# Four orders ahead of the first feed-forward product, and new priorities behind it, in a fused attention and Fourier-mixing kernel

## The chip, the cores and the metric

The kernel runs on one core of one Trainium2 chip. The metric is the device time of one execution in microseconds (us), lower is better. The core has four engines that compute side by side, TensorE (PE in the profile), VectorE (DVE), ScalarE (ACT) and GpSimd (POOL), and a fifth, SyncE (SP), which here only issues transfers. Each engine works through its own list of instructions in the order in which they were written; where one needs another's result, it waits on a semaphore.

## The reference

Eight batches of 448 tokens with 12 heads of 64. Cosine attention, then a Fourier mixing over tokens and channels of which only the real part is kept, then a layer norm and a two-layer feed-forward with a residual:

```python
q_n = q / (np.linalg.norm(q, axis=-1, keepdims=True) + 1e-06)
k_n = k / (np.linalg.norm(k, axis=-1, keepdims=True) + 1e-06)
scores = np.matmul(q_n, k_n.transpose(0, 1, 3, 2)) / tau        # tau = 0.1
attn = softmax(scores)
x = np.matmul(attn, v)            # heads joined: (8, 448, 768), float32
mixed = np.real(fft(fft(x, axis=1), axis=2))
u = x + mixed
un = (u - mean(u)) / np.sqrt(var(u) + 1e-06)
out = u + np.maximum(un @ w_ch1, 0.0) @ w_ch2     # 768 -> 3072 -> 768
```

## The kernel before

The whole program is written down first as a list of steps (`P.add`, each with its engine or engines to choose from, an estimated duration, a priority, what it reads and writes), and a planner (`Plan.schedule`) then deals the steps out: whenever an engine comes free it takes, of the steps that are ready by the planner's own clock, the one with the lowest priority number. The result is one fixed list per engine. In that list only true dependences become semaphore waits (`deps`). A second kind of relation, `order`, only says that one step may be dealt out after another has been; it sets places in the lists and never makes a wait.

A table `SHIFT` adds a number to the priority of single steps by name and occurrence (`"mask": {0: 513.4649}`). It was found by a search, so there is nothing to read in its numbers; their effect is the order of the lists.

The work of one batch b, with the names of its steps:

- Loads of q, k, v. Squares of q and k on ACT (`sqK`, `sqQ`, `sqT`; T is the tail of 64 tokens), their sums on DVE (`ssK`, `ssQ`, `ssT`), logarithm and exponential for the root on ACT (`ln`, `nrm`), and the scaling of q and k on DVE (`scK`, `scQ`, `scT`). For batches 0 and 1 the scaled tiles are transposed on PE (`tk`, `tq`, `tt`) through two PSUM banks (pool "M") and copied out on ACT or DVE (`ek`, `eq`, `et`). From batch 2 on POOL does the scaling and a transfer does the transposing.
- Scores on PE (`qk`), exponentials on ACT (`ex`), values on PE (`pv`), division on DVE (`rd`, `x`), folds of the token axis on DVE (`fa`, `f0`, `f1`, `g`).
- First Fourier product on PE (`fs0`, `fs1`), copied out (`te0` on ACT; for batch 0 `te1` is split, one half on ACT, one on DVE), second one on PE (`fd0`, `fd1`). The sine and cosine tables for it are made on ACT (`sind`), with `mask`, a small DVE step, behind it. In batch 0 the tables are brought into another shape afterwards (`cd0` to `cd5`, `halfd`).
- The residual sum `u` (`u0`, `u1`) for three token tiles on DVE, the tile's negative mean (`ba`), its sum of squares on ACT (`bs`), root (`ln2`, `rs`), the normed tile on DVE (`un`). In batch 0 the first tile is only centred (its root is applied at the very end), so that it needs `ba` but not `bs`. The tile is transposed on PE (`tn0`, in two halves) and copied out of PSUM in two halves (`eu00`, `eu01`).
- The first feed-forward product on PE (`h0` to `h23`, 6 matmuls each; for batch 0 first on the lone first tile, 144 matmuls of 128x128, then on a pair of tiles, 128x256), the ReLU out of pool "M" on ACT or DVE (`relu`), the second product on PE (`y`, and `m1` to `m7` in a form with fewer multiplications), the closing additions on DVE (`fin`), for part of the tiles as a copy on ACT (`fa`, `fv`, `fm`) and an addition on POOL (`fap`, `fvp`, `fmp`), the store by SP or POOL.

The attention of batch b+1 is interleaved with the feed-forward of batch b. PE's idle places before the first product are filled with matmuls whose result nobody reads (`warm`, 6 each). Two switches of ACT's function table stand near the first product: `ldt1` ahead of the sine tables and `ldt` behind them.

The functions that the change touches stand below, with the line numbers of the profile.

Of the kernel before, what the change touches and what calls it, by code (L numbers as in the profile page):

```python
# [86 lines left out]
    "pads": {0: 761.6515}, "sins": {0: 15.0098}, "ldt0": {0: 217.8585}, "ldt1": {0: -55.8965}, "sind": {0: 7.1264}, "mask": {0: 513.4649},  # L87
    "sinp": {0: 701.9659}, "half": {1: 12.0477}, "sinn": {0: -46.2638}, "ldt": {0: 60.769}, "sqK0_0": {0: -198.99}, "ssT0_0": {0: -143.0895},
# [778 lines left out]
def t_act(n, ptr=0):  # L867
    return 0.12 + 0.00089 * n + 0.093 * ptr


def t_dve(n, mode=1):
    return 0.1 + n / (960.0 * mode)
# [15 lines left out]
class Kern:  # L888
# [202 lines left out]
    def first_norm(self, b):  # L1091

        P = self.P
# [7 lines left out]
        if b == 0:  # L1101
            cuts = ((0, 1), (1, 3), (3, 6))
            hf = self.tf[:, 0:10752].bitcast(F32)
            sg = self.hf[:, 0:6144].bitcast(F32)
# [18 lines left out]
        pg = [pr + 1.5 * a for a, _ in cuts]  # L1123
# [1093 lines left out]
```

## Time and profile before

| what | value |
|---|---|
| time, median of 3 runs | 575.67 us (575.16 to 577.59) |
| the profiled execution | 574.34 us, its span 572.5 us |
| PE busy | 552.2 us, 96% of the span |
| DVE busy | 439.6 us, 77% |
| ACT busy | 382.8 us, 67% |
| POOL busy | 231.5 us, 40% |
| granted TensorE clock | 1.00 throughout |
| first feed-forward matmul starts | 48.46 us after the span's start |

A row of the timeline reads: start, length, engine, line, operation, what it writes and reads, and in brackets the idle time before it and who ended it. Rows of one form that follow each other are merged (x2), and their length is then from the first start to the last end. The time an engine is held by an instruction is a little shorter than its length: the next one may start before the last result is written.

### The profile page before, as it was taken

The page shows a single profiled execution, that of the slowest core. Times are in us where ns is not written, and L with a number is a line of the kernel's source. Part 1 is how long each engine was busy: PE and PEld are TensorE (multiplying, and loading weights), DVE is VectorE, ACT ScalarE, POOL GpSimd, SP SyncE. Part 2 cuts the span into 40 slices and gives each one's busy share as a digit, 9 for nine tenths or more (in the row PEclk, how much of TensorE's full clock was granted, in tenths as well). Part 3 has the DMA queues.
Part 4 walks back from the last instruction along what each step waited for, and adds up shares of the span by engine and source line. Part 5 has one row for each costly group of instructions (what it writes and reads, how often), then busy time and mean ns, then how long its engine had stood idle before and what let it go on. Part 6 is the DMA issues. An engine that isn't in the chain of part 4 may idle for free.

```text
span 572.5 us, 15993 instructions
## 1 busy us (share of the span) xinstructions
PE 552.2 (96%) x6598; PEld 432.6 (76%) x6598; DVE 439.6 (77%) x926; ACT 382.8 (67%) x723; POOL 231.5 (40%) x338
## 2 busy tenths in 40 slices
PE   3799999999999999999999999999999999999998
PEld 3569787686787678868778787687786886969695
DVE  8989857988488768886879668977986497987363
ACT  7898895565876676798458775696456752747171
POOL 8534424347345535453471536344532103031303
PEclk9999999999999999999999999999999999999999
DMA  9999998985349938953695549553933100023001
GB/s 193 210 239 174 170 181 123 161 180 109 113 68 114 171 87 126 138 125 92 121 125 109 83 109 132 116 128 54 142 65 34 62 1 26 32 41 73 21 36 56
DMA packets 187897, 62.19 MB, mean 109 GB/s; under 512 B 166800, under 2 KB 185616, under 8 KB 187824
## 3 DMA queue, kind: packets, MB, share of 16 engines
q1 hardware_dynamic: 129856, 38.35, 36.2%
q0 software_dynamic: 57968, 22.81, 36.0%
q8 instruction: 52, 0.85, 0.6%
q14 instruction: 21, 0.17, 0.1%
HBM read 51.90 MB, written 11.01 MB: 110 GB/s over the span
## 4 chain that ended last, share of the span: by engine, by line
PE 75%; DVE 17%; ACT 5%; issue 2%; POOL 1%; DMA 0%; DVEq 0%; POOLq 0%; ACTq 0%
PE PS L1902 26%; PE PS L1758 26%; PE PS L1853 6%; PE PS L1397 6%; PE PS L1360 5%; DVE U L1620 3%; DVE HQ L2002 2%; PE PS L1391 2%; ACT E L1338 2%; PE PS L1373 1%; DVE ACG L1609 1%; PE PS L1525 1%; DVE U L1632 1%; DVE OUTB L1939 1%; DVE SM L1272 1%
## 5 line engine op out<-in xcount | busy, mean ns | idle before, releaser
L1758 PE MATMUL PS<-UNT,W1b 128*128 128x256 bf16 (+1 forms) x1728 | 185.3, 264 | 1.2 <-ACT KTD L1230 0.4
L1758 PEld LDWEIGHTS PS<-UNT,W1b 128*128 128x128 bf16 x1728 | 154.0, 98 | 21.3 <-issue 1.7
L1338 ACT ACTIVATE E<-PS 128x900 bf16<-128x900 f32 (+1 forms) x192 | 149.3, 827 | 28.6 <-PE PS L1360 24.6
L1902 PE MATMUL PS<-W2b,HQ 128*128 128x384 bf16 x720 | 124.8, 326 | 0.0
L1283 POOL TENSOR_TENSOR QH<-STG,SM 128x256 bf16<-128x256 f32 x126 | 87.4, 720 | 90.9 <-DVE SM L1089 64.7
L1928 POOL TENSOR_TENSOR OUTB<-OUTB,U 128x192 f32<-128x192 f32 x72 | 50.8, 725 | 127.0 <-ACT OUTB L1923 125.8
L1902 PEld LDWEIGHTS PS<-W2b,HQ 128*128 128x128 bf16 x720 | 68.8, 98 | 43.3 <-issue 0.6
L1902 PE MATMUL PS<-TX,HQ 128*128 128x384 bf16 (+2 forms) x444 | 76.7, 322 | 1.6 <-DVE OUTB L1939 1.4
L1774 ACT ACTIVATE HQ<-PS 128x512 bf16<-128x512 f32 x82 | 48.8, 597 | 37.9 <-PE PS L1758 37.0
L1902 PEld LDWEIGHTS PS<-TX,HQ 128*128 128x128 bf16 x444 | 41.4, 98 | 28.2 <-DVE OUTB L1939 2.5
L2002 DVE TENSOR_TENSOR HQ<-HQ 128x1536 bf16<-128x1536 bf16 (+1 forms) x73 | 55.1, 758 | 9.1 <-ACT HQ L1774 6.3
L1272 DVE TENSOR_REDUCE SM<-QH 128x6 f32<-128x384 f32 x84 | 45.1, 544 | 13.1 <-ACT QH L1270 12.5
L1397 PE MATMUL PS<-VB,E 128*128 128x65 bf16 x1152 | 51.9, 193 | 0.0
L1270 ACT ACTIVATE QH<-STG 128x384 f32<-128x384 f32 x84 | 43.0, 521 | 10.3 <-DVE SM L1272 9.5
L1397 PEld LDWEIGHTS PS<-VB,E 128*128 128x128 bf16 x1152 | 47.9, 97 | 1.5
L1961 POOL DMA_INDIRECT out_dram<-OUTB,IDX x21 | 23.4, 1115 | 57.5 <-DVE OUTB L1939 30.1
L1774 DVE TENSOR_SCALAR HQ<-PS 128x512 bf16<-128x512 f32 x44 | 30.1, 684 | 19.7 <-PE PS L1758 19.1
L1391 PE MATMUL PS<-VZ,E 128*128 128x130 bf16 x192 | 41.6, 219 | 1.0 <-ACT E L1338 0.9
L1662 ACT ACTIVATE F<-U,MV 128x768 bf16<-128x768 bf16 x28 | 26.2, 934 | 21.2 <-DVE MV L1657 17.8
L1620 DVE SCALAR_TENSOR_TENSOR U<-ACG,X 128x768 bf16<-128x768 f32 (+4 forms) x39 | 39.3, 1014 | 0.7
L1360 PE MATMUL PS<-QK 64*128 64x225 bf16 (+2 forms) x864 | 39.1, 227 | 0.1
L1923 ACT ACTIVATE OUTB<-PS 128x384 f32<-128x384 f32 x36 | 17.6, 488 | 29.5 <-PE PS L1902 29.2
(193 smaller groups left out, 784.3 us busy)
## 6 DMA issues: line engine op xcount, KB each, us to landing
STG<-in_k_dram SPq DMA_DIRECT2D x18, 384.0 KB, 4.6
STG<-in_q_dram SPq DMA_DIRECT2D x18, 384.0 KB, 3.7
VB<-in_v_dram POOLq DMA_DIRECT2D x24, 192.0 KB, 6.7
W1b<-in_moe_w_ch_dram POOLq DMA_DIRECT2D x12, 384.0 KB, 8.0
W2b<-in_moe_w_ch_dram POOLq DMA_DIRECT2D x12, 384.0 KB, 6.7
out_dram<-OUTB SPq DMA_DIRECT2D x7, 384.0 KB, 4.4
W2b<-in_q_dram SPq DMA_DIRECT2D x2, 576.0 KB, 10.1
W2b<-in_k_dram SPq DMA_DIRECT2D x2, 576.0 KB, 11.0
```

Of the source, the lines that this page charges most:

```text
L1272: P.add("dve", lambda v, o=SS[:, i, H // ns * x:H // ns * (x + 1)], sq=sq: v.tensor_reduce(o, sq.rearrange("p (h d) -> p h d", d=DH), AX.X ...
L1283: r = v.tensor_tensor(v3(qh)[:, h:h + 4], v3(buf)[:, h:h + 4], RN[:, i, h:h + 4].unsqueeze(2).to_broadcast((128, 4, DH)), AluOp.mult)
L1338: return a.activation(o, self.PS[:, bk:bk + nc_, 0:SQ2], ACTF.Exp, scale=1.0 / self.tau)
L1360: i = pe.matmul(self.PS[:, bk + h, c0:c0 + n], self.KT[r, jj, kt * 128:(kt + 1) * 128], self.QT[r, jj, cols], start=True, stop=True)
L1391: r = pe.matmul(o, st(6), self.VZ[:, j, :], start=not split, stop=(split and i == 0), skip_group_check=True)
L1397: r = pe.matmul(o[:, 65 * h:65 * h + 65], st(2 * kt + h), self.VB[:, kt, 2 * j + h, :], start=(split and i == h == kt == 0), stop=((not sp ...
L1620: self.snu.append(P.add("dve", lambda v: v.scalar_tensor_tensor(two(U[o0:o0 + n, ut, :]), src, 1.0, two(X[i0:i0 + n, x, :]), AluOp.mult, A ...
L1758: r = pe.matmul(self.PS[:, bk, x * n:(x + 1) * n], self.W1b[:, j, ft * 128:(ft + 1) * 128], self.UNT[:, j, cs], start=(j == 0), stop=(j == ...
L1774: return e.activation(o, i, ACTF.Relu) if e is self.nc.scalar else e.tensor_relu(o, i)
L1902: r = pe.matmul(self.PS[:, bk, 0:n], lhs(f), rhs(f), start=(start and f == 0), stop=(stop and f == NF // 2 - 1), skip_group_check=True)
L1928: r = g.tensor_tensor(self.OUTB[:, ob, xs], self.OUTB[:, ob, xs], self.U[:, ut, xs], AluOp.add)
L2002: P.add("dve", lambda v: v.tensor_tensor(cs(o), cs(a), cs(bq), op), 0.16 + 0.3 * len(ks), -0.5, f"{nm}{ks[0]}_{b}", reads=rd, writes=[x fo ...
```

## The change

Four orders are laid on the planner, all around the first product, and the `SHIFT` table was searched anew, so that priorities everywhere else differ too:

1. The squares of batch 1's k and tail (not those of q) are dealt out after `te1`'s ACT half; the table switch `ldt` too. The sums of these squares are dealt out after the copies `eu00` and `eu01`.
2. The third and all later additions of `u` in batch 0 are dealt out after the first tile's centring `un0`.
3. The first tile's squares `bs0`, and `cd2` to `cd5`, are dealt out after `eu00` and `eu01`.
4. In batch 0 the four halves of `fd` are dealt out in the order in which they are written.

```diff
-... "mask": {0: 513.4649},
+... "mask": {0: -82.2081},
...
-  t_act(w), pg[g], f"sq{nm}{g}_{b}", reads=names, writes=sqn[g][i], order=[self.exps[-1]] if b else [])
+  t_act(w), pg[g], f"sq{nm}{g}_{b}", reads=names, writes=sqn[g][i], order=[self.exps[-1]] + self.te[1:] * (i != 1) if b else [])
...
-  ..., f"ss{nm}{g}_{b}", reads=sqn[g][i], writes=[...], order=sc if b else []))
+  ..., f"ss{nm}{g}_{b}", reads=sqn[g][i], writes=[...], order=sc + self.un0 * (i != 1) if b else []))
...
+            if es == ("act",):
+                self.te.append(te)
...
-  tiles=(tile,), acquire=tile if sg or b else None, margin=0.2))
+  tiles=(tile,), acquire=tile if sg or b else None, margin=0.2, order=self.fd_ops[-1:] if b == 0 else ()))
...
+                if late:
+                    bs.order = tuple(bs.order) + tuple(P.ops[-2:])
+                    self.un0 = P.ops[-2:]
+                    for u in [x for x in self.snu[2:] if x.name == "u0_0"] + [x for x in self.snu if x.name == "u1_0"]:
+                        u.order = tuple(u.order) + (un,)
+                    for x in P.ops:
+                        if x.name in ("cd2", "cd3", "cd4", "cd5"):
+                            x.order = tuple(x.order) + tuple(self.un0)
+                    self.ldt.order = tuple(self.ldt.order) + tuple(self.te)
```

Line numbers of the changed kernel are 31 higher up to the scaling code and 33 to 42 higher behind it.

ACT's list between the tables and the first product, before. `CS<-UNT,MV` and `TX<-U` are `sind`, `E<-PS` are `te0` and `te1`, `OUTB<-W2b` are squares of batch 1, `CS<-CS` are `cd`, `F,MV<-U,MV` is `bs0`, `UNT<-PS` is a half of `eu0`:

```order
L1034 ACTIVATE TX<-U 128x770
L1546 ACTIVATE E<-PS 128x2x450
L1146 ACTIVATE OUTB<-W2b 128x1152
L1546 ACTIVATE E<-PS 65x450
L1053 ACT_TABLE_LOAD
L1146 ACTIVATE OUTB<-W2b 128x384
L2100 ACTIVATE CS<-CS 97x2x97
L1662 ACTIVATE F,MV<-U,MV 128x768
L1691 ACTIVATE UNT<-PS 128x3x128
```

The same place now:

```order
L1065 ACTIVATE TX<-U 128x770
L1577 ACTIVATE E<-PS 128x2x450
L1577 ACTIVATE E<-PS 65x450
L1084 ACT_TABLE_LOAD
L1177 ACTIVATE OUTB<-W2b 128x1152
L2142 ACTIVATE CS<-CS 97x2x97
L1724 ACTIVATE UNT<-PS 128x3x128
L2142 ACTIVATE CS<-CS 97x2x96
L1724 ACTIVATE UNT<-PS 128x3x128
L1695 ACTIVATE F,MV<-U,MV 128x768
```

The large square moved behind `te1` and the table switch, `bs0` behind the copies, and both halves of the copy are ACT's now, with one `cd` between them.

DVE's list at the same time, before. `SM<-W2b` and `SM<-OUTB` are sums of squares, `E<-PS` is the DVE half of `te1`, `MV<-TX` is `mask`, `U,ACG<-PS,X` are the additions of `u`, `MV<-ACG` is `ba0`, `F<-U,MV` are the two halves of `un0`, `UNT<-PS` is `eu00`:

```order
L1149 TENSOR_REDUCE SM<-W2b 128x3x6
L1547 CAST E<-PS 65x450
L1149 TENSOR_REDUCE SM<-OUTB 128x3x6
L1045 TENSOR_SCALAR MV<-TX 128x1
L1632 SCALAR_TENSOR_TENSOR U,ACG<-PS,X 128x384 x2
L1658 TENSOR_SCALAR MV<-ACG 128x1
L1632 SCALAR_TENSOR_TENSOR U,ACG<-PS,X 128x384
L1674 TENSOR_SCALAR F<-U,MV 128x384 x2
L1632 SCALAR_TENSOR_TENSOR U,MV<-PS,X 64x384
L1691 CAST UNT<-PS 128x3x128
```

And now:

```order
L1076 TENSOR_SCALAR MV<-TX 128x1
L1180 TENSOR_REDUCE SM<-W2b 128x3x6
L1578 CAST E<-PS 65x450
L1665 SCALAR_TENSOR_TENSOR U,ACG<-PS,X 128x384 x2
L1691 TENSOR_SCALAR MV<-ACG 128x1
L1707 TENSOR_SCALAR F<-U,MV 128x384 x2
L1665 SCALAR_TENSOR_TENSOR U,MV<-PS,X 64x384
L1665 SCALAR_TENSOR_TENSOR U,ACG<-PS,X 128x384
L1180 TENSOR_REDUCE SM<-OUTB 128x3x6
```

The sum of k's squares and the third addition moved behind `un0`, `mask` moved ahead of the sum of q's squares, and `eu00` is gone from DVE.

DVE some 8 us later, before, where the second and third tile are normed. `MV<-ACG` is `ba2`, `F<-U,MV` of 128x768 are `un1` and `un2`, `L1172` and `L1168` are scalings of batch 1:

```order
L1658 TENSOR_SCALAR MV<-ACG 128x1
L1089 RECIPROCAL SM<-SM 128x42
L1674 TENSOR_SCALAR F<-U,MV 128x768
L1172 TENSOR_TENSOR TX<-W2b,SM 128x384 x2
L1168 TENSOR_TENSOR TX<-W2b,SM 128x128 x2
L1172 TENSOR_TENSOR QH<-W2b,SM 128x384
L1674 TENSOR_SCALAR F<-U,MV 128x768
```

And now:

```order
L1120 RECIPROCAL SM<-SM 128x42
L1691 TENSOR_SCALAR MV<-ACG 128x1
L1203 TENSOR_TENSOR QH<-W2b,SM 128x384 x3
L1203 TENSOR_TENSOR TX<-W2b,SM 128x384 x3
L1707 TENSOR_SCALAR F<-U,MV 128x768 x2
L1199 TENSOR_TENSOR TX<-W2b,SM 128x128 x3
```

All six large scalings now stand ahead of both norms.

PE behind the centred first tile, before. `UNT,W1b 128x128` are `h` of the lone tile, `TX,F` are `tn1` and `tn2`, `TX,QH` are `tk`, `TX` of 128x128 x3 with 128x64 and 128x1 is a `tq`:

```order
L1758 MATMUL PS<-UNT,W1b 128x128 x120
L1683 MATMUL PS<-TX,F 128x128 x6
L1758 MATMUL PS<-UNT,W1b 128x128 x12
L1207 MATMUL PS<-TX 128x128 x3
L1208 MATMUL PS<-TX 128x64
L1209 MATMUL PS<-TX 128x1
L1758 MATMUL PS<-UNT,W1b 128x128 x12
L1683 MATMUL PS<-TX,F 128x128 x6
L1195 MATMUL PS<-TX,QH 128x128 x6
```

And now:

```order
L1800 MATMUL PS<-UNT,W1b 128x128 x144
L1226 MATMUL PS<-TX,QH 128x128 x3
L2198 MATMUL PS<-W1b 128x128 x6
L1226 MATMUL PS<-TX,QH 128x128 x3
L1716 MATMUL PS<-TX,F 128x128 x6
L1226 MATMUL PS<-TX,QH 128x128 x3
L1716 MATMUL PS<-TX,F 128x128 x6
```

The 144 matmuls run through, and both norms' transposes stand behind them, between transposes of k.

POOL in batch 1's feed-forward, before (`QH<-STG,SM` are three instructions for one scaling of a later batch, `OUTB<-OUTB,U` two for one closing addition):

```order
L1283 TENSOR_TENSOR QH<-STG,SM 128x256 x6
L1961 DMA out_dram<-OUTB,IDX 3584x768
L1283 TENSOR_TENSOR QH<-STG,SM 128x256 x6
L1928 TENSOR_TENSOR OUTB<-OUTB,U 128x192 x2
L1283 TENSOR_TENSOR QH<-STG,SM 128x256 x3
L1928 TENSOR_TENSOR OUTB<-OUTB,U 128x192 x4
L1283 TENSOR_TENSOR QH<-STG,SM 128x256 x6
```

And now:

```order
L1314 TENSOR_TENSOR QH<-STG,SM 128x256 x6
L2003 DMA out_dram<-OUTB,IDX 3584x768
L1314 TENSOR_TENSOR QH<-STG,SM 128x256 x9
L1970 TENSOR_TENSOR OUTB<-OUTB,U 128x192 x6
L1314 TENSOR_TENSOR QH<-STG,SM 128x256 x6
```

One scaling moved ahead of the first addition. At most later places of all lists the order differs in this way, by one or a few steps; the number of matmuls and of `warm` groups is the same.

More of the change, by code (lines that the diff above doesn't have):

```diff
@@ L1146, in first_norm @@
                 P.add("act", lambda e, sq=sq, buf=buf: e.activation(sq, buf, ACTF.Square), t_act(w), pg[g], f"sq{nm}{g}_{b}",
-                      reads=names, writes=sqn[g][i], order=[self.exps[-1]] if b else [])
+                      reads=names, writes=sqn[g][i], order=[self.exps[-1]] + self.te[1:] * (i != 1) if b else [])
                 out = SS.rearrange("p (j c) -> p j c", c=14)[:, a:a + n, 6 * i:6 * i + (6, 6, 2)[i]]
                 red.append(P.add("dve", lambda v, sq=sq, out=out, n=n: v.tensor_reduce(out, sq.rearrange("p (j h d) -> p j h d", j=n, d=DH), AX.X, AluOp.add),
-                                 t_dve(w), pg[g], f"ss{nm}{g}_{b}", reads=sqn[g][i], writes=[f"SS_{a + j}{i}" for j in range(n)], order=sc if b else []))
+                                 t_dve(w), pg[g], f"ss{nm}{g}_{b}", reads=sqn[g][i], writes=[f"SS_{a + j}{i}" for j in range(n)], order=sc + self.un0 * (i != 1) if b else []))
             self.norms(b, pg[g], 14 * a, 14 * (a + n), [f"SS_{a + j}{i}" for j in range(n) for i in range(3)], rn[0] + rn[1] + rn[2])
@@ L1548, in fsum @@
             n_ = len(ah) * SQ2
-            P.add(es, ev, [t_act(n_) if e == "act" else t_dve(n_) for e in es], pj, f"te{blk}_{b}",
+            te = P.add(es, ev, [t_act(n_) if e == "act" else t_dve(n_) for e in es], pj, f"te{blk}_{b}",
                   writes=[f"Tt{blk}" + ("b" if len(ah) == 1 and ah[0] else "")], after=[tile.users[0], self.pvs[-1 if b == 0 and blk == 0 else -2]], tiles=(tile,))
+            if es == ("act",):
+                self.te.append(te)
     def fft(self, b):
@@ L1661, in fft @@
             ns_ = 3 if late else nb_
[L1662 removed]
+            bs = P.add("act", lambda a, ut=ut, ns_=ns_, mean=mean, var=var: a.activation(
                 self.UN[:, ns_, :], U[:, ut, 0:DM], ACTF.Square, bias=mean, accum_out=var),
@@ L2112, in build @@
         self.stg_next = self.qh_next = self.ln_next = self.out_next = 0
-        self.trs, self.loads, self.ssk, self.fd_ops, self.w, self.raw1, self.vl, self.pvs, self.exps = [], [], [], [], [], [], [], [], []
+        self.trs, self.loads, self.ssk, self.fd_ops, self.w, self.raw1, self.vl, self.pvs, self.exps, self.te, self.un0 = [], [], [], [], [], [], [], [], [], [], []
         self.first_st = self.main = self.last_qk = self.ldt = None
```

5 lines of the change are left out of this document (2 added, 3 removed), and 903 rows, old and new, of the table SHIFT.

## Prediction

> **What bounds the kernel now.** I read the busy times in five stretches first, cut at the starts of the second Fourier product (43.81), the first product of the lone tile (48.46), and the first product of the pair (62.21), then PE's waits behind the last cut, then the timeline of each engine around the first product.
>
> ```profile
> 0.00:43.81 43.81, 30.78 (x456) 23.31 (x456) 38.65 (x88) 37.93 (x60) 24.93 (x55) 1.00 1.31 213
> 43.81:48.46 4.65, 4.14 (x52) 3.68 (x51) 4.50 (x15) 3.48 (x7) 2.01 (x3) 1.00 1.25 164
> 48.46:62.21 13.75, 12.64 (x198) 11.36 (x199) 13.39 (x39) 12.54 (x31) 8.45 (x11) 1.00 1.34 173
> 62.21:190.00 127.79, 127.21 (x1319) 97.06 (x1319) 98.14 (x203) 86.69 (x165) 56.98 (x76) 1.00 1.02 137
> 190.00:573.00 383.00, 377.44 (x4576) 297.16 (x4576) 284.91 (x585) 242.19 (x463) 139.16 (x195) 1.00 0.54 84
> ```
>
> (After the stretch's length: PE, weight loads, DVE, ACT, POOL busy, with their instructions; the granted clock.) PE is the bound behind 62.21: of 127.79 us it works 127.21. Between 48.46 and 62.21 it lacks 13.75 - 12.64 = 1.11 us. Ahead of 48.46 DVE and ACT are the busier ones (38.65 and 37.93 of 43.81), so there the time is set by their lists. The change adds no work to PE, so it can gain only by starting PE's full stretch earlier and by removing waits in it. These are the waits behind 62.21 (its first row but three, KTD, is the one at 62.21 itself and belongs to the stretch ahead):
>
> ```profile
> PE PS L1902 <- DVE OUTB L1939: 1.4, 2, 1.0
> PE PS L1521 <- DVE F L1485: 0.7, 1, 0.7
> PE PS L1758 <- ACT KTD L1230: 0.4, 1, 0.4
> PE PS L1758 <- DVE MV L1657: 0.3, 1, 0.3
> PE PS L1758 <- DMA UNT<-F: 0.3, 1, 0.3
> PE PS L1902 <- DVE HQ L2002: 0.3, 1, 0.3
> PE PS L1853 <- DMA UNT<-F: 0.2, 1, 0.2
> ```
>
> Without KTD they sum to 3.2 us. That is all that the new priorities can take away behind the first stage.
>
> **The change part by part: up to the first product.** ACT, DVE and PE in the timeline:
>
> ```profile
> 40.64 0.83 ACT L1034 ACTIVATE TX<-U 128x770 bf16<-128x770 f32 x1
> 41.38 0.90 ACT L1546 ACTIVATE E<-PS 128x900 bf16<-128x900 f32 x1
> 42.18 1.15 ACT L1146 ACTIVATE OUTB<-W2b 128x1152 f32<-128x1152 f32 x1
> 43.23 0.53 ACT L1546 ACTIVATE E<-PS 65x450 bf16<-65x450 f32 x1
> 43.78 1.28 ACT L1053 ACT_TABLE_LOAD   x1
> 45.07 0.52 ACT L1146 ACTIVATE OUTB<-W2b 128x384 f32<-128x384 f32 x1
> 46.75 0.37 ACT L2100 ACTIVATE CS<-CS 97x194 bf16<-97x194 bf16 x1 [1.15 <-PE PS L1568]
> 47.02 0.92 ACT L1662 ACTIVATE F<-U,MV 128x768 bf16<-128x768 bf16 x1
> 47.94 0.47 ACT L1691 ACTIVATE UNT<-PS 128x384 bf16<-128x384 f32 x1
> ```
>
> ```profile
> 41.34 1.34 DVE L1149 TENSOR_REDUCE SM<-W2b 128x18 f32<-128x1152 f32 x1
> 42.60 0.61 DVE L1547 CAST E<-PS 65x450 bf16<-65x450 f32 x1
> ...
> 45.39 0.56 DVE L1632 SCALAR_TENSOR_TENSOR U<-PS,X 128x384 bf16<-128x384 f32 x1
> ...
> 45.99 0.21 DVE L1658 TENSOR_SCALAR MV<-ACG 128x1 f32<-128x1 f32 x1
> 46.12 0.55 DVE L1632 SCALAR_TENSOR_TENSOR U<-PS,X 128x384 bf16<-128x384 f32 x1
> ...
> 46.59 0.58 DVE L1674 TENSOR_SCALAR F<-U,MV 128x384 bf16<-128x384 bf16 x2
> ```
>
> ```profile
> 41.48 0.98 PE L1525 MATMUL PS<-CS,ACG 128*65 128x225 bf16 x8
> ...
> 43.81 0.34 PE L1568 MATMUL PS<-TX,E 128*128 128x193 bf16 x2
> ...
> 47.01 0.56 PE L1683 MATMUL PS<-TX,F 128*128 128x128 bf16 x6 [0.30 <-DVE F L1674]
> ...
> 48.46 6.90 PE L1758 MATMUL PS<-UNT,W1b 128*128 128x128 bf16 x120 [0.22 <-ACT UNT L1691]
> ```
>
> *Squares behind the copies.* `fs1` ends at 41.48 + 0.98 = 42.46, but `te1` on ACT starts at 43.23, behind the square of 42.18, and `fd` starts at 43.81, right behind `te1`'s end (43.23 + 0.53 = 43.76). With the square gone `te1` runs from about 42.50 to 43.03. Then DVE's half is the later one. It ends at 42.60 + 0.61 = 43.21 today, and now `mask` stands ahead of it, which reads what the sine table at 40.64 writes until 41.47: it starts at 41.51, the sum of q's squares at 41.60 instead of 41.34, and the cast ends at 43.47. So `fd` starts at 43.51, 0.30 earlier. `mask` costs about 0.26 of the 0.55 that was there.
>
> *Third addition.* `ba0` follows at 45.69 for 45.99. Today `un0` starts at 46.59, behind the addition of 46.12; now it waits for `ba0`'s result alone, 0.21 + 0.04: 45.94, 0.65 earlier in all. `tn0` (today 47.01) starts at 46.36 and has both halves out at 46.92.
>
> *First tile's squares.* Today the copy at 47.94 waits for the 0.92 of `bs0`. Now ACT does `cd0` at 46.45 for 0.27 (46.75 to 47.02 is what it holds ACT), `eu00` at 46.74 to 47.11, `cd1` to 47.38, `eu01` to 47.85. A copy of 0.47 has moved from DVE to ACT with a `cd` between, which takes back some 0.4 us of the squares' 0.9. The first product starts at 47.9 for 48.46: **0.55 us earlier**.
>
> The table switch moves from 43.78 to 43.03. It holds ACT for 45.07 - 43.78 = 1.29, which is over at 44.33, and the large square then ends at 45.48, ahead of `cd0`; so it is hidden, with 0.97 to spare. [...]
>
> Weights for the product: the issues on POOL ahead of it are the same in both lists, and the last of w_ch1 leaves at 48.17 and lands 6.6 later.
>
> ```profile
> 48.17 0.82 POOL L1066 DMA_DIRECT2D W1b<-in_moe_w_ch_dram  x1 [1.28 <-DMA W1b<-in_moe_w_ch_dram]
> ```
>
> ```profile
> DMA to landing us min/median/max: 6.6/6.6/6.6
> ```
>
> That is 54.8; it is needed at product 132 of 144, 47.9 + 132 x 6.90 / 120 = 55.5. Covered by 0.7.
>
> **To the pair's first product.** The steps that PE does between the two marks are the same set in both lists, so its start compares cleanly (62.21). Today the second and third tile's norms and a scaling stand in DVE's timeline so:
>
> ```profile
> 54.97 0.38 DVE L1674 TENSOR_SCALAR F<-U,MV 128x768 bf16<-128x768 bf16 x1
> 55.26 1.02 DVE L1172 TENSOR_TENSOR TX<-W2b,SM 128x384 bf16<-128x384 f32 x2
> ...
> 57.08 0.47 DVE L1674 TENSOR_SCALAR F<-U,MV 128x768 bf16<-128x768 bf16 x1
> ```
>
> Now six scalings of 0.47 (1.02 for two, less the overlap) stand ahead of both, 2.8 us: with `ba2` near 54.8, `un1` runs at 57.6 and `un2` at 57.9. PE meets this late: it has 144 products to do first, until 47.9 + 8.28 = 56.2, then `tk0`, a warm group and `tk2`, 57.0. There it waits for `un1`, or for the bank of `tk2`, which ACT frees only behind `bs1`, `bs2` and their roots; about 1.3 us. Against that, today's waits in this stretch (1.11) lie elsewhere and mostly go, since the scalings are then done. The sides: all 1.11 go and no new one comes, -0.55 - 1.11 = -1.66; or 1.3 come on top of today's, +0.75. Walking ACT's and DVE's rows of today along the new lists gives 61.8 to 62.0 for 62.21. I take **-0.4**.
>
> **Behind it.** Of the 3.2 us of waits the new lists plainly change one. At 292.42 PE waits 0.37 for the closing addition:
>
> ```profile
> 292.42 0.82 PE L1902 MATMUL PS<-TX,HQ 128*128 128x384 bf16 x4 [0.37 <-DVE OUTB L1939]
> ```
>
> There the next batch's first Fourier product now stands ahead of that matmul, and covers it. At the largest wait, POOL's chain is the same as before: two scalings, then four instructions of closing additions, then DVE, then PE:
>
> ```profile
> 186.72 2.99 POOL L1928 TENSOR_TENSOR OUTB<-OUTB,U 128x192 f32<-128x192 f32 x4
> ```
>
> ```profile
> 190.44 1.80 PE L1902 MATMUL PS<-TX,HQ 128*128 128x384 bf16 x10 [1.01 <-DVE OUTB L1939]
> ```
>
> So I keep it and the others: **-0.4**. The ends: -3.2 if all go; +3.2 as an estimate for lists that make as many new waits as the old ones have.
>
> **Sum.** -0.4 - 0.4 = -0.8 (the 0.55 of the first product is inside the first). The profiled execution took 574.34, its span 572.5 and 1.84 around it; it would take 573.5. It lies 1.33 below the median of the runs shown, so against the median: 575.67 - 0.8 = **574.9 us**.
>
> **Rivals.** *Faster.* The early waits vanish and the new priorities remove about half of the later ones: -0.55 - 1.11 - 1.6 = -3.3, 572.4. For it: PE's list is free of other limits behind 62.21. Against: at the largest wait nothing changes, and DVE's backlog of 2.8 us is visible in the list.
>
> *Slower: POOL's additions.* A closing addition on POOL frees the bank that product `m5` takes. In batch 1 a scaling, three instructions, now stands ahead of the first one:
>
> ```profile
> 138.11 2.26 POOL L1283 TENSOR_TENSOR QH<-STG,SM 128x256 bf16<-128x256 f32 x3 [0.17 <-POOL OUTB L1928]
> ```
>
> If the addition stands ready and the scaling runs first, it is 2.26 late. Here POOL was idle just before, so that I expect 0 to 0.4; but where POOL has no slack the whole 2.26 reaches PE. Two such places outweigh the 0.8 and 2.9 more: 575.67 - 0.8 + 4.5 = 579.4. Against: at other places additions have moved ahead of scalings.
>
> *The orders do nothing.* They set places, not waits; `un1`'s backlog and the banks hand back all of the 0.55, and the later waits stay: 575.7.
>
> *The clock.* It was granted in full (1.00) in all stretches, also in the first, where PE lacks 13 of 43.81 us. A halving behind the new wait near 57 could at most double what PE does from there to 62.21, about 4 us: 575.67 - 0.8 + 4 = 578.9. [...]
>
> **Chances.** My forecast 0.60 (between -2.5 and +2.0), faster 0.20, POOL's additions 0.10, nothing 0.08, the clock 0.02. Runs of this kernel spread over 0.4%, and about 0.5% (2.9 us) is what a measurement can tell from no change. Below 572.8: most of the faster rival, 0.18. Above 578.6: most of the POOL rival, 0.09. Within: 0.73. The range runs from 572.0, inside the faster rival, to 577.5, which takes in my forecast's upper end and stops short of POOL's and the clock's; about 0.08 and 0.12 stay outside.
>
> **What would show it.** The first 128x128 product near 47.9 with both copies of the transposed tile on ACT; `fd` behind DVE's cast, not ACT's, near 43.5; PE waiting up to 1.3 us near 57 for DVE's norm or ACT's copy; the pair's first product between 61.5 and 62.3; the wait of 1 us in batch 1's last product still there, that of 292 gone. Wrong, if the pair's first product starts before 61 or after 63, or if PE's waits behind it sum to under 1.5 or over 5 us.

## The result, and the profile after

The changed kernel took 578.33 us (median of 14 executions, 577.18 to 580.19) against 575.53 for the kernel before beside it; the ratio is 1.0051 [1.0041, 1.0061]. It is slower by 2.8 us, outside the range that was predicted. The profiled execution took 577.47, its span 575.7.

The stretches again, cut at the same steps (columns: the stretch's length, then PE, weight loads, DVE, ACT and POOL busy, each with its instructions, then the granted clock):

```profile
47.57:61.83 14.26, 12.90 (x204) 11.63 (x204) 13.91 (x40) 13.31 (x32) 8.06 (x10) 1.00 1.26 165
61.83:190.00 128.17, 126.75 (x1313) 96.13 (x1314) 100.74 (x202) 86.01 (x165) 58.39 (x75) 1.00 0.90 135
190.00:576.00 386.00, 378.24 (x4584) 298.03 (x4582) 284.52 (x583) 244.77 (x467) 142.80 (x198) 1.00 0.50 84
```

PE's work is the same (6598 matmuls in both). Between the pair's first product and 190 it is idle for 1.42 us where it was idle for 0.58. The clock is 1.00 everywhere. PE's waits behind the pair's first product (engine, line, whom it waited for: sum, times, longest):

```profile
PE PS L1552 <- DVE F L1516: 2.0, 2, 1.1
PE PS L1944 <- DVE MV L1690: 1.8, 2, 1.4
PE PS L1944 <- DVE OUTB L1981: 1.0, 1, 1.0
PE PS L1422 <- ACT E L1369: 0.4, 1, 0.4
PE PS L1800 <- DVE UNT L1724: 0.2, 1, 0.2
PE PS L1556 <- DVE F L1516: 0.2, 1, 0.2
PE PS L1800 <- DVE OUTB L1981: 0.2, 1, 0.2
```

Without the row of `UNT`, which is the wait at 61.83 itself, they sum to 5.6 us, where there were 3.2. In the first row PE twice, at 295.33 and 482.80, reaches a sine product (`fs1`, L1552) before its input, DVE's last fold (L1516), is there; the one wait of 0.7 that the kernel before has in this row is another batch's, at 356, and is gone. The second row holds the wait at 190, now 1.43, and one of 0.33 at 248. The row of 1.0 is a product that waits for a closing addition (L1981). Of the waits of before, three are gone, at 356, 373 and 434 (0.66, 0.30 and 0.25). Timelines say where, and the start of the same product in both traces says what it cost. In the table below both are counted from the first Fourier product `fs0` (38.35 before, 37.93 after; PE's and ACT's lists are the same up to it). The number is how much later than in the kernel before the product starts:

| product, its start before | after | old_133_new | mend_four | old_133_mended |
|---|---|---|---|---|
| first product, 48.46 | -0.47 | 0.04 | -0.47 | 0.04 |
| pair's first product, 62.21 | 0.04 | -0.06 | 0.36 | 0.12 |
| `h23` of the pair, 89.69 | 0.78 | -0.05 | 1.10 | 0.13 |
| `m10` of batch 1, 133.26 | 1.06 | -0.05 | 1.38 | 0.13 |
| behind the place at 140 | 2.27 | 1.72 | 1.38 | 0.24 |
| `qk50` of batch 3, 214.57 | 2.39 | 2.14 | 1.79 | 0.36 |
| last third of `m70` of batch 3, 289.29 | 2.77 | 2.55 | 2.16 | 0.72 |
| behind the place at 294, 302.28 | 3.46 | 3.25 | 1.85 | 0.42 |
| behind the place at 450, 456.79 | 2.07 | 1.98 | -0.11 | -0.98 |
| behind the place at 481, 502.31 | 3.41 | 3.32 | 0.21 | -0.65 |
| `m42` of the last batch, 568.79 | 2.99 | 2.90 | -0.20 | -1.07 |

(The three right-hand columns are experiments, told below. Ahead of each product PE has done the same steps in all columns, fillers apart, but for `h23` in the columns after and mend_four: `qk4t`, about 0.2, now stands ahead of it.) The first product is earlier as forecast, the pair's first product is not. Then the time goes in steps: 1.0 up to 133, 1.2 at 140, 0.5 from there to 289, 0.7 at 294, 1.3 at 481; between 302 and 457 the new lists win 1.4 back, and 0.4 after 502.

**Up to the first product.** PE and ACT:

```profile
43.17 0.33 PE L1601 MATMUL PS<-TX,E 128*128 128x193 bf16 x2
...
47.57 0.62 PE L1800 MATMUL PS<-UNT,W1b 128*128 128x128 bf16 x8 [0.38 <-ACT UNT L1724]
```

```profile
42.64 1.28 ACT L1084 ACT_TABLE_LOAD   x1
43.93 1.17 ACT L1177 ACTIVATE OUTB<-W2b 128x1152 f32<-128x1152 f32 x1
46.14 0.37 ACT L2142 ACTIVATE CS<-CS 97x194 bf16<-97x194 bf16 x1 [1.04 <-issue]
46.41 0.47 ACT L1724 ACTIVATE UNT<-PS 128x384 bf16<-128x384 f32 x1
46.78 0.36 ACT L2142 ACTIVATE CS<-CS 97x192 bf16<-97x192 bf16 x1
47.03 0.48 ACT L1724 ACTIVATE UNT<-PS 128x384 bf16<-128x384 f32 x1
```

Both copies of the transposed tile (`UNT<-PS`) stand on ACT, with a `cd` ahead of each, as the order showed.

**To the pair's first product.** PE, then DVE:

```profile
55.39 0.84 PE L1800 MATMUL PS<-UNT,W1b 128*128 128x128 bf16 x12 [0.19 <-DMA W1b<-in_moe_w_ch_dram]
56.57 0.34 PE L1226 MATMUL PS<-TX,QH 128*128 128x128 bf16 x3 [0.34 <-ACT TX L1816]
...
61.83 0.39 PE L1800 MATMUL PS<-UNT,W1b 128*128 128x256 bf16 x2 [0.23 <-DVE UNT L1724]
```

```profile
54.65 1.50 DVE L1203 TENSOR_TENSOR QH<-W2b,SM 128x384 bf16<-128x384 f32 x3
56.06 1.49 DVE L1203 TENSOR_TENSOR TX<-W2b,SM 128x384 bf16<-128x384 f32 x3
57.47 0.86 DVE L1707 TENSOR_SCALAR F<-U,MV 128x768 bf16<-128x768 bf16 x2
```

The earlier first tile runs into a landing of the weights, a ReLU, and the six scalings ahead of the two norms. The landing is late because its transfer is: POOL issued it at 48.63, which is 49.05 on the clock of before, for 48.17 there, and it landed 6.7 later.

**The place at 140.** POOL, DVE and PE after:

```profile
136.01 3.69 POOL L1314 TENSOR_TENSOR QH<-STG,SM 128x256 bf16<-128x256 f32 x3 [0.17 <-POOL QH L1314]
139.85 1.05 POOL L1970 TENSOR_TENSOR OUTB<-OUTB,U 128x192 f32<-128x192 f32 x2
```

```profile
135.43 3.80 DVE L2044 TENSOR_TENSOR HQ<-HQ 128x1536 bf16<-128x1536 bf16 x3
140.93 0.56 DVE L1981 TENSOR_TENSOR OUTB<-PS,OUTB 128x384 f32<-128x384 f32 x1 [1.70 <-POOL OUTB L1970]
```

```profile
141.55 0.82 PE L1944 MATMUL PS<-TX,HQ 128*128 128x384 bf16 x4 [1.04 <-DVE OUTB L1981]
```

and before, POOL's addition there:

```profile
136.04 1.90 POOL L1928 TENSOR_TENSOR OUTB<-OUTB,U 128x192 f32<-128x192 f32 x2 [0.61 <-ACT OUTB L1923]
```

The scaling `sc0` of the batch after next now stands ahead of POOL's addition `fa0p`, and takes 3.69 where the same three instructions took 2.26 behind it. DVE adds three times 1536 columns meanwhile. The addition comes out at 140.9, DVE's closing addition behind it, and PE, with `m50` next in its list, waits.

**The place at 294.** Before, DVE's two additions of 764 columns and POOL's next additions:

```profile
287.48 1.03 DVE L1468 TENSOR_TENSOR ACG<-F 128x764 bf16<-128x764 bf16 x2
...
289.30 3.00 POOL L1928 TENSOR_TENSOR OUTB<-OUTB,U 128x192 f32<-128x192 f32 x4
```

After, the same two, and PE's product behind them:

```profile
289.09 2.17 DVE L1499 TENSOR_TENSOR ACG<-F 128x764 bf16<-128x764 bf16 x2
...
289.74 1.10 POOL L1970 TENSOR_TENSOR OUTB<-OUTB,U 128x192 f32<-128x192 f32 x2
...
295.33 1.03 PE L1552 MATMUL PS<-CS,F 128*97 128x113 bf16 x16 [0.94 <-DVE F L1516]
```

Two of POOL's four additions have moved ahead of its last load of values and so fall on DVE's two. DVE's take 1.14 longer, about what POOL's two take (1.10), and `fs1`, moved ahead of `m40` in PE's list, waits for the chain that they begin. With POOL's two behind the load again (`pool_three`, below) DVE's take 1.38; why that is not 1.03, no run here shows. At 136 both engines' operations were longer: the scaling took 3.69 for 2.26, and DVE's three additions 3.80 for 0.94 and 2.38.

**The place at 481.** PE and DVE:

```profile
482.80 1.03 PE L1552 MATMUL PS<-CS,F 128*97 128x113 bf16 x16 [1.09 <-DVE F L1516]
```

```profile
481.52 1.22 DVE L1516 TENSOR_TENSOR F<-F 128x388 bf16<-128x388 bf16 x2
```

Here `fs1` of the last batch stands ahead of a third of `m70`. Before, it stood 13 steps further back, among the products `p` of the next tile, and did not wait. A smaller wait is at 450, where a product of values waits for an exponential of ACT with `h0`, which needs none of it, behind it in the list:

```profile
450.62 0.23 PE L1422 MATMUL PS<-VZ,E 128*128 128x130 bf16 x1 [0.40 <-ACT E L1369]
```

### The profile page after: what moved, and what is told of

Its sections match the earlier page's. It is cut to its first block, busy times and chain, and to the rows that moved or that the text cites. A ratio compares the mean times of both kernels' runs of the same rounds, so it can differ in the third digit from the quotient of the medians.

```text
span 575.7 us, 15991 instructions
## 1 busy us (share of the span) xinstructions
PE 552.9 (96%) x6598; PEld 432.6 (75%) x6598; DVE 440.9 (77%) x922; ACT 384.8 (67%) x727; POOL 235.9 (41%) x338
## 3 DMA queue, kind: packets, MB, share of 16 engines
q1 hardware_dynamic: 129856, 38.35, 33.7%
## 4 chain that ended last, share of the span: by engine, by line
PE 61%; DVE 4%; POOL 0%; ACT 0%; issue 0%; POOLq 0%; ACTq 0%
PE PS L1944 21%; PE PS L1800 21%; PE PS L1895 7%; PE PS L1428 4%; PE PS L1391 3%; PE PS L1422 1%; PE PS L1404 1%; DVE HQ L2044 1%; DVE OUTB L1981 1%; PE PS L1552 1%; PE PS L1611 1%; DVE F L1512 1%; DVE U L1653 0%; DVE ACG L1499 0%; POOL OUTB L1970 0%
## 5 line engine op out<-in xcount | busy, mean ns | idle before, releaser
L1314 POOL TENSOR_TENSOR QH<-STG,SM 128x256 bf16<-128x256 f32 x126 | 92.7, 761 | 81.7 <-DVE SM L1120 78.4
L1816 ACT ACTIVATE HQ<-PS 128x512 bf16<-128x512 f32 x85 | 50.6, 596 | 37.0 <-PE PS L1800 36.1
L2044 DVE TENSOR_TENSOR HQ<-HQ 128x1536 bf16<-128x1536 bf16 (+1 forms) x73 | 53.4, 734 | 8.7 <-PE PS L1944 4.0
L1816 DVE TENSOR_SCALAR HQ<-PS 128x512 bf16<-128x512 f32 x41 | 28.2, 688 | 20.7 <-PE PS L1800 20.6
L1346 POOL DMA_DIRECT2D VB<-in_v_dram x24 | 25.4, 1064 | 32.9 <-PE PS L1428 19.6
```

What stands on the lines that cost most here:

```text
L1314: r = v.tensor_tensor(v3(qh)[:, h:h + 4], v3(buf)[:, h:h + 4], RN[:, i, h:h + 4].unsqueeze(2).to_broadcast((128, 4, DH)), AluOp.mult)
L1816: return e.activation(o, i, ACTF.Relu) if e is self.nc.scalar else e.tensor_relu(o, i)
L2044: P.add("dve", lambda v: v.tensor_tensor(cs(o), cs(a), cs(bq), op), 0.16 + 0.3 * len(ks), -0.5, f"{nm}{ks[0]}_{b}", reads=rd, writes=[x fo ...
```

## The experiments

All use the changed kernel's steps and their true waits. Except in one (`orders_alone`) the planner's dealing is replaced by five fixed lists of step names, one for each engine. The lists hold the steps in the order of the changed kernel or of the one before (neither was run by itself in this form). So one step can be moved, or a kernel can follow one plan up to a named step and the other plan from there. A step is written as name and batch: `sc0_3` is the scaling `sc0` of batch 3. Each result is the median and the ratio to the kernel before that ran beside it, with its 95% interval. That kernel's median lay between 574.83 and 575.53 in the different sittings, so kernels of different sittings are compared by the ratio; it is not always the ratio of the two medians (in `pool_three` these give 1.0040, the ratio on record is 1.0054).

**Early lists against late lists.** Two kernels swap the plan at the pair's first product.

```diff
 early_new_late_old: new lists up to h0 of the pair, old lists behind
 early_old_late_new: old lists up to h0 of the pair, new lists behind
```

> The changed kernel's five instruction lists up to and with the pair's first product, then the lists of the kernel before. Theory T1 (the loss lies in a few places behind the pair's first product, each with one step placed ahead of what TensorE waits for): 574.7 to 575.4, ratio 0.998 to 1.000, the pair's first product near 61.8 and TensorE's waits behind it back to those of before (1.2 us near 190, about 0.5 near 292, no wait over 0.5 near 140 or 481). Rival T2 (the early stage hands on a backlog, six scalings and the late first tile, that costs later): over 577.5, ratio over 1.003. Rival T3 (VectorE and GpSimd slow each other everywhere, no single place): between, near 576.5.

> The reverse: the lists of the kernel before up to and with the pair's first product, then those of the changed kernel. T1: 578 to 579, ratio 1.004 to 1.006, with the waits near 140, 190, 294 and 481 as in the changed kernel. T2: 575 to 576, ratio near 1.000. T3: near 577.

Measured: 576.11, 1.0017 [1.0008, 1.0026], and 578.16, 1.0065 [1.0048, 1.0082]. The late lists carry the larger part, as the first theory (T1) has it. But the early lists cost 1 us by themselves, which it had not (576.11 is nearer to what T3 gave), and the two come to more than the 1.0051 of both. In the first kernel the planner had put 18 filling products behind the pair's first product; without them:

> The changed kernel's lists up to the pair's first product and the old ones behind, as in the earlier run, but without the 18 filling products that the planner put behind the pair's first product there (63.63 to 64.73, 1.1 us of TensorE). T1: those 18 were what made the earlier one slower, so 574.6 to 575.3, ratio 0.999 to 1.001. T2 (the early stage hands on a backlog): still over 1.0015.

Measured: 577.28, 1.0038 [1.0023, 1.0052]. A miss: in place of the fillers PE waits 0.69 for ACT's exponentials. The new early lists hand ACT on late (its first exponential starts at 61.95 after, 60.94 before, 1.4 later when both are counted from `fs0`, behind a square of 1.16), so T2 holds a part where the old lists follow.

**The new lists up to 51 us alone.**

```diff
 new_to_51: new lists up to h10 of the first tile, old lists behind
```

> The changed kernel's lists up to 51 us (the first tile's product h10), the old ones from there on. T1: the first product is 0.47 earlier, and the gain was used up between 51 and 62 by the six scalings ahead of the later normalisations and the late scale of the second tile; with the old lists there the pair's first product comes 0.3 to 0.5 earlier too: 574.4 to 574.7, ratio 0.999. Rival T4 (the pair's start is held by landings of the weights and by steps that did not get earlier): pair's start as before, ratio 1.000 or above.

Measured: 574.89, 0.9993 [0.9984, 1.0003]. In its trace the first product is 0.47 earlier and the pair's is 0.75 later, after a wait of 0.71 for a ReLU that the old DVE list has later. Alone the earlier first product is worth nothing that can be measured.

**The orders without the search.**

```diff
 orders_alone: the four orders as in the diff
-SHIFT table of the changed kernel
+SHIFT table of the kernel before; the planner deals anew
```

> The four orders ahead of the first product with the table of priorities as before; the planner deals the later steps anew. T1 has the later lists as the place of the loss, so this kernel's time is set by which later places its own lists leave open: first product about 0.5 earlier as in the changed kernel, and the total by the sum of its own later waits, 573 to 579. T2: over 577.5 whatever the later waits are.

Measured: 671.63, 1.1679 [1.1664, 1.1694]. Neither theory had that. The row is of its groups by line: matmuls whose result nobody reads, of which the kernel before has 6 at this line.

```profile
L2167 PE MATMUL PS<-W1b 128*128 128x128 bf16 x1464 | 93.9, 219 | 3.8 <-DVE SM L1272 0.6 <-DVE OUTB L1950 0.6 <-DVE SM L1089 0.3
```

The table is fitted to one plan. With four orders added the planner foresees gaps all over and fills them, 94 us in all. The orders cannot be judged by themselves through this planner.

**One step on GpSimd's list.**

```diff
 pool_back, GpSimd: ... sc5_2 sc6_2
-sc0_3 fa0p_1
+fa0p_1 sc0_3
```

> The changed kernel with one thing moved: on GpSimd's list the scaling sc0 of batch 1's first round stands behind the addition fa0p again, as before the change. T1: the 1.20 us wait of TensorE ahead of the projection's product m5 at 140 goes to under 0.2, and the time falls by 0.9 to 1.3, to 577.0 to 577.4 (ratio to the kernel before about 1.003). T3: the wait goes but another takes its place, or the time falls by less than 0.4.

Measured: 577.38, 1.0041 [1.0028, 1.0054]. The wait at 140 is gone: `m10` of batch 1 and the step behind the place are both 1.44 late, where the changed kernel went from 1.06 to 2.27. By the ratio it brings about 0.6, not 0.9 to 1.3, and the intervals overlap; the wait at 190 grew by 0.3, and the early part of this execution was later.

**Two and six places put back.**

```diff
 mend_two, TensorE at 294 (a name repeated is the next third of the product)
-m30_3 fs1_4 fs0_4 m40_3 m40_3
+m30_3 m40_3 fs1_4 fs0_4 m40_3
 VectorE at 294
-e0_4 e1_4 ss6_5 fin11_3
+e0_4 fin11_3 e1_4 ss6_5
 TensorE at 481
-m70_6 fs1_7 fs0_7 m70_6 m30_6 m30_6 fd0_7 m30_6
+m70_6 m70_6 m30_6 fs1_7 fs0_7 m30_6 m30_6 fd0_7
 mend_six: mend_two, pool_back, and on TensorE
 at 69 tq3_1, tk3_1, tq5_1 one to three steps later
 at 98 fs1_1 and fs0_1 behind y011
 at 450 h0_6 ahead of pv20_7
```

> The changed kernel with two places of the later part put back as they stood before relative to their neighbours: near 294 the sine products fs1 and fs0 of batch 4 behind the first third of m40 on TensorE, and the output fin11 ahead of the second combination e1 on VectorE; near 481 fs1, fs0 and fd0 of batch 7 behind m30's thirds. T1: the waits of 1.1 and 1.25 us go, 0.5 stays at the first: the time falls by 1.4 to 2.0, to 576.3 to 577.0, ratio about 1.002 to 1.003. T3 (spread-out slowing): other waits take their place, the time stays over 577.6.

> As the two-place kernel, with four more: near 69 the transposes of raw squares tq3, tk3, tq5 of batch 1 two steps later on TensorE, near 98 the sine products of batch 1 behind y011, at 140 the scaling sc0 behind the addition on GpSimd, near 450 the product h0 ahead of pv20. T1: the waits of 0.67, 0.36, 1.2 and 0.57 us go as well: 574.3 to 575.5, ratio 0.999 to 1.001. T3: over 576.5.

Measured: 577.47, 1.0031 [1.0019, 1.0043], and 577.32, 1.0033 [1.0021, 1.0045]. By the ratio the first lies at the edge of what T1 gave, the second in the range of T3. The move at 481 works (from 457 to 502 us the loss is 0.32 in place of 1.34). The move at 294 does not: PE now waits for the closing addition instead:

```profile
297.80 0.82 PE L1684 MATMUL PS<-TX,HQ 128*128 128x384 bf16 x4 [1.13 <-DVE OUTB L1721]
```

So DVE itself is late there, whatever PE has first. The move at 69 made a new wait of 1.28, for DVE's reciprocal `rd`. What makes DVE late can stand on GpSimd's list there.

**Three moves on GpSimd, and two on TensorE besides.**

```diff
 pool_three, GpSimd: pool_back, and at 187
-sc5_3 sc6_3 fv2p_1 fm2p_1
+sc5_3 fv2p_1 fm2p_1 sc6_3
 at 290
-fv0p_3 ld_v2_5 fm0p_3
+ld_v2_5 fv0p_3 fm0p_3
 mend_five: pool_three and the moves on TensorE at 450 and 481
```

> The changed kernel with three moves, all on GpSimd's list: at 140 the scaling sc0 behind the addition fa0p; near 187 the additions fv2p and fm2p ahead of the second of two scalings (sc6); near 290 the addition fv0p of batch 3 behind the last load of values. Theory T5 (TensorE's large waits behind the pair's start come from what stands on GpSimd's list next to VectorE's work): the 1.2 at 140 goes, the 1.6 to 1.9 at 190 falls under 0.7, VectorE's two additions of 764 columns near 289 take 1.0 to 1.1 in place of 2.17 and the wait behind them falls from 1.1 to under 0.6: 575.6 to 576.6, ratio 1.000 to 1.002. T3 (spread out, other waits come up): over 577.

> As the kernel with three moves on GpSimd, and two on TensorE: near 481 the sine products fs1, fs0 and fd0 of batch 7 behind m30's thirds, near 450 the product h0 ahead of pv20. The two were worth 1.0 and 0.4 in the kernels that had them: T1: 574.2 to 575.4, ratio 0.998 to 1.000, so that all of what the change lost is named. T3: over 576.

Measured: 577.35, 1.0054 [1.0033, 1.0075], and 576.71, 1.0029 [1.0015, 1.0042]. As totals both are misses, in the range of T3. At 290 the move did most of what T5 said: DVE's two additions take

```profile
290.19 1.38 DVE L1239 TENSOR_TENSOR ACG<-F 128x764 bf16<-128x764 bf16 x2
```

in place of 2.17, and from `m70` to 302 us the kernel gains 0.29 where the changed one loses 0.69. At 187 it failed. The wait of `m42` at 190 falls to 0.09, but the next products wait:

```profile
193.83 0.76 PE L1131 MATMUL PS<-QK 64*128 64x225 bf16 x12 [1.43 <-issue]
195.22 1.07 PE L1540 MATMUL PS<-UNT,W1b 128*128 128x128 bf16 x13 [0.64 <-DMA UNT<-F]
```

SyncE's queue says why. The transfer that transposes what `sc6` scaled is issued later, and the transfers of the normed tile stand behind it in the same queue (the first is issued at 192.44 here, 190.53 in the changed kernel). In `pool_three` the granted clock fell to 0.60 behind these waits too (below); in `mend_five` it did not (mean over the profiled execution 1.0).

**The middle stretch alone.**

```diff
 new_341_407: old lists, but the new ones from pv40 of batch 5 to m70 of batch 5
 mid_190: new_341_407, and fv2p_1, fm2p_1 ahead of the second scaling on GpSimd
```

> The lists of the kernel before, with those of the changed kernel between 341 and 407 us alone (from the product pv40 of batch 5 to m70 of batch 5), where the changed kernel's products gain 2.5 us on those of before. T1 (a stretch's lists carry its time): 573.0 to 574.2, ratio 0.995 to 0.998. Rival T6 (the gain there was slack that the later arrival had bought, so it is not to be had alone): 575 or more, ratio over 0.999.

> As the kernel with the changed lists between 341 and 407 alone, and on GpSimd's list the two additions fv2p and fm2p near 187 ahead of the second scaling, so that VectorE's addition fin31 and TensorE's m42 near 190 come 1 us earlier. T1 and T5: 0.6 to 1.2 below that kernel, 572.0 to 573.4. T3: no difference from it.

Measured: 576.75, 1.0031 [1.0021, 1.0042], and 584.38, 1.0157 [1.014, 1.0173]. The first doesn't tell its theories apart, since the cut itself did harm: ACT has a ReLU behind a square whose data have not landed, and PE waits

```profile
348.74 1.62 PE L1540 MATMUL PS<-UNT,W1b 128*128 128x256 bf16 x8 [3.89 <-ACT HQ L1556]
```

The second shows the failure at 187 again, larger: PE waits 2.0 and then 5.2 for the transfers behind the late scaling.

**The four places that paid.** The changed kernel with the moves at 140 and 290 on GpSimd and at 450 and 481 on TensorE, and nothing at 187; and the same late lists with old early ones.

```diff
 mend_four, GpSimd
-sc0_3 fa0p_1
+fa0p_1 sc0_3
 ...
-fv0p_3 ld_v2_5
+ld_v2_5 fv0p_3
 TensorE: h0_6 ahead of pv20_7; fs1_7, fs0_7, fd0_7 behind thirds of m30_6
 old_133_new:         old lists up to m10 of batch 1, new lists behind
 old_133_mended:      old lists up to m10 of batch 1, mend_four's behind
 new_51_133_mended:   new lists up to h10, old ones up to m10 of batch 1, mend_four's behind
```

> The changed kernel with the four places mended (140, 290, 450, 481) and nothing else. T1: 3.0 to 3.6 less than the changed kernel and what the early stage lost is kept: 575.0 to 576.2, ratio 1.000 to 1.002. T3: over 577.

> The lists of the kernel before up to 133 us (batch 1's projection m10), those of the changed kernel from there. In the trace of the changed kernel 1.06 of its 2.99 us were lost ahead of this point and 1.93 behind it. T1 (two parts that add up, about a third early and two thirds late): 576.5 to 577.6, ratio 1.0025 to 1.0045. T2 (the early stage decides): under 576.

> As the one with the old lists up to 133, and with the four places mended that paid in earlier runs: at 140 and 290 on GpSimd's list (sc0 behind fa0p, fv0p behind the last load), at 450 and 481 on TensorE's. Worth in traces 1.2, 1.0, 0.35 and 1.0. T1: 3.0 to 3.6 less than without them, 573.0 to 574.6, ratio 0.996 to 0.9995, faster than both kernels. T3 (other waits come up): 575.5 or more.

> As the mended one with the old lists up to 133, but with the changed kernel's lists ahead of 51 us, the old ones from 51 to 133. If the first product's 0.47 is worth something to the end, 0.3 to 0.6 below that kernel; if it is used up by 62 us, equal to it within 0.3.

| kernel | median, us | ratio to before |
|---|---|---|
| the changed kernel | 578.33 | 1.0051 [1.0041, 1.0061] |
| old_133_new | 577.75 | 1.0052 [1.0040, 1.0064] |
| mend_four | 574.73 | 1.0002 [0.9992, 1.0011] |
| new_51_133_mended | 574.89 | 1.0003 [0.9993, 1.0012] |
| old_133_mended | 573.60 | 0.9985 [0.9975, 0.9994] |

(The first row is of another sitting than the four below it.) The last is faster than both kernels. `mend_four` leaves out nothing and moves six steps, and the whole loss is gone in the total: 2.2 us are still lost up to 289, and the new lists win as much back behind it. Its waits behind the pair's first product:

```profile
PE PS L1684 <- DVE MV L1430: 2.1, 2, 1.7
PE PS L1296 <- DVE F L1256: 0.2, 1, 0.2
PE PS L1540 <- DVE OUTB L1721: 0.2, 1, 0.2
```

`old_133_new` was a miss, 577.75 for at most 577.6: without the early loss of 1.06 the time is no better. The table above shows it. At 140 it loses 1.77 where the changed kernel loses 1.21, since PE comes earlier and GpSimd does not:

```profile
143.13 0.82 PE L1684 MATMUL PS<-TX,HQ 128*128 128x384 bf16 x4 [1.42 <-DVE OUTB L1721]
```

With the four places mended, the early lists do count: old ones 0.9985, new ones 1.0002, about 1 us. `new_51_133_mended` is a miss in both its branches, 1.3 us slower than `old_133_mended` and no faster than `mend_four`, though it has new lists up to 51 us alone. Its trace says where: at 133 it is 0.31 late for 0.13, and from 289 to 302 it loses 0.30 where `old_133_mended` wins 0.30. There DVE's two additions reach into POOL's again, which start at 290.35:

```profile
288.76 1.77 DVE L1239 TENSOR_TENSOR ACG<-F 128x764 bf16<-128x764 bf16 x2
```

In `old_133_mended`, with the same lists there, they take 1.39. So in these two traces the larger part of the difference is one of arrival at the place at 294, and not of work ahead of 133.

**An earlier start of the pair.**

```diff
 mend_four_eu, VectorE
-ek1_1 ssK1_1 et0_1 eu11_0
+ek1_1 eu11_0 et0_1 ssK1_1
 old_133_mended_kt, ScalarE
-ex0_1 et0_1
+et0_1 ex0_1
 VectorE
-ssK1_1 et0_1
+et0_1 ssK1_1
```

> The changed kernel with the four places mended, and one more move on VectorE: the sum of squares ssK1 of batch 1 (1.34 us, ahead of the copies that the pair's first product waits for) behind the copies eu11 and et0. If the pair's start is held by that VectorE list, its first product comes 0.6 to 1.2 earlier, near 60.9 on the clock of the mended kernel's 62.2, and at least half of it is kept: 573.8 to 574.5, ratio 0.998 to 0.9995. If it is held by later copies on ScalarE or the sums of squares are then late for the raw squares near 69, no difference within 0.4 from 574.7.

> The fastest so far (the old lists up to 133, the changed ones with four places mended behind) with the copies et0 of batch 1, for which the pair's first product waits there, ahead of the exponential ex0 on ScalarE and ahead of the sum of squares ssK1 on VectorE. Pair's first product 0.4 to 0.8 earlier; if the exponentials have that much slack, 572.8 to 573.3, ratio 0.997 to 0.998; if they have none, equal to 573.6 within 0.3.

Measured: 576.87, 1.0029 [1.0017, 1.0041], and 575.22, 1.0001 [0.9991, 1.0010]. Both slower than without the move. In both the pair's first product comes 0.5 earlier against its neighbour, and more is lost at once. In the second:

```profile
61.49 0.81 PE L1540 MATMUL PS<-UNT,W1b 128*128 128x256 bf16 x6 [0.17 <-DVE KTD L1001]
...
65.97 1.26 PE L1540 MATMUL PS<-UNT,W1b 128*128 128x256 bf16 x10 [1.09 <-DVE HQ L1556]
```

A ReLU (HQ) on DVE is late now, behind the sum of squares that was moved. In the first, ACT's next square waits 1.13 for that sum, and the exponentials behind it are late.

## Why the prediction was wrong, step by step

- **First product, -0.55: right.** It measured -0.47 from `fs0`, with each mechanism in its place: `fd` at 43.17 (43.59 on the clock of before, for 43.51), both copies on ACT. The table load shows 1.29 to the next square again (42.64 to 43.93).
- **Weights covered by 0.7: wrong by about 1.** PE waited 0.19 for the landing (0.35 from start to start). The issues are the same, as the prediction said, but the last one started 0.88 later on the clock of before, behind a wait of POOL for earlier landings; the prediction had kept its old time.
- **Pair's first product, -0.4: wrong by 0.4.** It started at 61.83, inside the range given, but 0.42 of that is where this execution began. From `fs0` it is +0.04. The backlog of six scalings was there and took 2.82 for 2.8. (In the prediction's list of waits `KTD`, the one at the pair's start, is the third row.) PE is idle for 1.36 in this stretch (14.26 - 12.90), where 1.3 was the forecast, but that the sum fits is luck: only 0.38 of it is for the scalings and the norm, the rest for the landing (0.19), a ReLU (0.34) and two copies (0.21 and 0.23). And PE's steps in it are not the same set, as the prediction has it: it does 204 matmuls for 198, one group of fillers more, 0.26 of work. So -0.47 - 1.11 + 1.36 + 0.26 = +0.04. Whether PE would have stood as long without the fillers no run shows; a wait for the norm follows them (0.16 at 58.00). With the same early lists other executions had the pair's start 0.03 to 1.00 late, so a single trace doesn't settle 0.4.
- **From the pair's start to 133 us: missing.** PE loses 1.0 there, in small pauses. The larger ones are near 69, where transposes of batch 1 have moved ahead in its list (0.16 at 68.63 and 0.26 at 69.89, from start to start; in `early_old_late_new` the same two wait 0.23 for a scaling on DVE and 0.25 for a copy), and 0.20 at 98.52 for DVE's last fold; the rest has no row of its own. ACT's exponentials start late here too, but need not be the cause: `early_old_late_new` has its first one at 60.88, as before, and loses 1.3 between the same two points. The prediction stopped at the pair's start as if only old waits counted from there on.
- **"Behind it", -0.4: the step that failed.** It measured +2.95. The wait at 292 was to be covered by the Fourier product now ahead of it; that product itself waits (0.94), since POOL's additions fell on DVE's. In the old trace it had no slack to be moved ahead: the fold that it needs ended at 293.10 and it started at 293.16. The wait at 190 stayed, as said (1.43 for 1.01). The others were kept, but three of them went (1.21 in all), which is most of the 1.4 won between 302 and 457. And no new ones were looked for: I asked of each old wait whether it stays, and not of each step moved ahead in PE's list whether its input would be there. The new ones are those at 140, 294, 450 and 481 (1.04, 0.94, 0.40 and 1.09), 0.33 at 248 and 0.20 at 98. `fs1` of batches 4 and 7 could be seen in the order; the change of GpSimd's list at 290 too, but not its price.
- **The rival of POOL's additions: right place, wrong price.** I expected 0 to 0.4, since POOL was idle ahead of it; it was 1.21. POOL's idle time ahead of the addition was 0.61 in the old trace and is gone in the new, and the scaling grew from 2.26 to 3.69 beside DVE's additions. With the place at 290 (0.69 lost, 0.31 won once mended) POOL's additions hold somewhat over half of what the four moves gave back. It had a chance of 0.10.
- **The clock: right.** 1.00 in every stretch. The halving that this rival reckons with stands in no trace of the two kernels; in `mid_190` the granted clock was 0.50 from 201.37 to 205.00 us, behind a wait of PE of 5.21, while the longest wait near 57 here was 0.34.
- **The sign that it is wrong** held: 5.6 us of waits, over 5.

What is not settled: why equal early lists give starts of the pair 1 us apart in single executions, and whether the new lists between 302 and 457 would win alone what they win there. That their gain is only slack bought by a late arrival (T6) does not fit `old_133_mended`: it comes to 302 only 0.42 late and is 0.98 ahead of the kernel before at 457.

## What to carry to other kernels

Where a change deals a whole list anew, go through every step that has moved ahead on the bounding engine and ask whether its input is ready, and not only through the waits that the old trace has. An engine off the path can set prices that its own list doesn't show: here DVE's two additions took 2.17 with two of POOL's beside them, 1.03 before. An earlier start at one point was worth nothing measurable here (`new_to_51`) while later places had waits of their own; with four of those mended, old against new early lists made 1 us.

## What was not expected of the hardware

- The same two DVE additions of 764 columns took 1.03 (`before`) and 1.38 (`pool_three`) where POOL only issued loads beside them, 1.77 (`new_51_133_mended`, `old_133_mended_kt`) where it reached its additions 0.18 before they ended, and 2.17 (the changed kernel) where two of its additions lay within them. In `old_133_mended_kt` and `old_133_mended` the lists there are the same and only the arrival differs, and it is 1.77 and 1.39.
- The granted clock fell behind long waits of PE: 0.55 over the next 3.26 us behind the one of 3.89. The row is of `new_341_407`, its tenth number the clock:

```profile
348.74:352.00 3.26, 3.26 (x17) 2.42 (x18) 3.12 (x8) 1.99 (x5) 0.00 (x0) 0.55 1.92 137
```

- In `pool_three` two waits of 1.43 and 0.64 within 3.6 us were followed by the same, 0.60 over the next 4 us, though PE worked 1.54 of the 3.60. In `mend_five` two waits of 1.42 and 0.66 at the same place left it at 1.00, and so did single waits of 1.73 and 1.88 at 190 (`mend_four`, `mend_four_eu`; the mean over each of these three profiled executions is 1.0, 0.997 in `pool_three`); what decides between the first two, no run here shows. The rows are of `pool_three`:

```profile
192.40:196.00 3.60, 1.54 (x26) 1.31 (x26) 2.56 (x8) 2.40 (x5) 2.25 (x2) 0.97 0.82 167
196.00:200.00 4.00, 4.00 (x45) 4.00 (x44) 1.49 (x3) 2.02 (x5) 0.27 (x1) 0.60 1.08 270
```
